# Q, K, V and output projections as column tiles beside PV, in a one-core transformer block (adaLN, sliding-window attention, gMLP)

## The chip, the cores and the metric

The kernel runs on one core of a Trainium2 chip. The metric is the time of one execution in microseconds (us); three runs of the kernel before took 271.88, 272.19 and 272.67 us, median 272.19.

A core has five engines that work side by side and wait for each other by semaphores: PE multiplies matrices (and loads their stationary operand, shown as PEld), ACT evaluates functions and copies, DVE and POOL work elementwise, SP issues most of the DMA transfers. A matmul streams the columns of a moving operand past a stationary one and writes sums into one of eight banks of an accumulator, `ps`; ACT and DVE copy results out. The 128 x 128 array can also be used in parts: row tiles (here four of 32 rows, of which 28 are used) or column tiles (four of 32 columns), each with its own stationary operand.

## The reference

The input x has 2048 rows of 448. With six vectors made from the condition c:

```
mod = silu(c) @ w_mod                      # sa, ca, ga, sb, cb, gb
h = layernorm(x) * (1 + ca) + sa
q, k, v = split(h @ wqkv)                  # 16 heads of 28
p = softmax(q @ k.T / sqrt(28), over the last 256 keys up to the row itself)
x = x + ga * ((p @ v) @ wo)
h = layernorm(x) * (1 + cb) + sb
z1, z2 = halves of gelu(h @ w_in)          # 896 + 896
g = w_sp @ layernorm(z2) + b_sp            # 2048 x 2048 over the rows
out = x + gb * ((z1 * g) @ w_out)
```

Inputs and output are bfloat16, sums are float32.

## The kernel before, in words

**Tiling.** The rows are cut into 16 tiles of 128. Attention goes tile by tile: tile j needs the keys of tiles j-2, j-1 and j. For each pair (tile, key tile) there are 16 score matmuls (one per head; four heads at a time as row tiles, `s_mm`, L806), two exponentials of 128 x 1024 on ACT (L841, one for half of the heads each), a mask on POOL for the first and last key tile (L847), and 16 PV matmuls as column tiles (`pv_fn`, L852, 128 rows x 32 columns, a column of ones in `Vaug` gives the softmax's sum). Then DVE transposes and normalises (L873 to L882), and `wo` multiplies (L889, result added to x at L892).

**Before attention.** The rows are normalised (L557 to L579), transposed to `hT` (blocks 0 to 2, that is tiles 0 to 3, by PE with an evacuation that applies the modulation, L629 to L648; the others by DMA, L663) and modulated. `project` (L719) computes Q and K transposed, eight groups of four heads per block, with `WQK` as the stationary operand and `hT` as the moving one, and V with `hT` as the stationary one, in chains of four steps over 448 = 4 overlapping chunks of 128 (rows that stand twice are zero in one of the chunks, L506 and L507). `WQK` has 32 columns for every head of 28, so that each head's Q and K land at a multiple of 32 partitions; eight copies (L679 on DVE, L680 on ACT) make it out of the loaded `wqk_raw`.

**After it.** LN and modulation again (`h2`), z1 and z2 by `w_in` with gelu (`Pair`, L684; rests of 64 rows as two row tiles at L711), the large product G (L1027, 448 matmuls of 512 columns), the elementwise product (L1037, L1039), `w_out` and the sum `fin` (L1059), one store per tile (L1061). The `w_in` products fill PE during attention where its order has room, and the rest of them follows. `w_sp` comes transposed by DMA (L1008); its second half overwrites `Vaug` and `PT` and waits for the last PV.

**Start.** The loads of c, x, w_mod, wqkv stand at L472 to L493; PE runs 30 matmuls on zeros (`warm`, L1068) so that it is busy before there is data. `mod_cols` (L526) makes sa and ca as 8 columns with four steps each, for which both halves of `w_mod` (L476) have to be there.

**Order.** No engine reorders its work: the program lists every operation, and `ORDER` (L164) gives the one order in which all are emitted, with a bank or buffer after "/" and the engine after "." where there is a choice. Each engine executes its own operations in that order, and `emit` (L102) puts in the waits. All matmuls but one kind go through `mm` (L438), so the profile shows nearly all of PE's work under L439.

Of the kernel before, what the change touches and what calls it, by code (L numbers as in the profile page):

```python
# [5 lines left out]
BF16 = mybir.dt.bfloat16  # L6
# [5 lines left out]
SWITCH = 95  # L12
# [43 lines left out]
class Planner:  # L56


    def __init__(self):
        self.ops = []  # L60
        self.last = {}
        self.order = []

# [15 lines left out]
    def schedule(self):  # L79
# [20 lines left out]
        assert len(self.order) == len(set(o.seq for o in self.order)) == len(self.ops)  # L100

    def emit(self, sems, dma_sems):  # L102
# [17 lines left out]
        for o in self.order:  # L120
# [18 lines left out]
            if o.dma is not None:  # L139
                dcount[name] = dcount.get(name, 0) + 16  # L140
                tok = ("dma:" + name, dcount[name])
                prog[eng].append(("op", o.fn, tok[0], 16))
                dlast[name] = tok
            else:
                cnt[eng] += 1
                tok = (eng, cnt[eng])
                prog[eng].append(("op", o.fn, eng, 1))
# [6 lines left out]
    def run(self, eng, e):  # L154
        for item in self.prog[eng]:
            if item[0] == "wait":
                e.wait_ge(self.sems[item[1]], item[2])
            else:
                _, fn, key, inc = item
                fn(e).then_inc(self.sems[key], inc)  # L160
# [4 lines left out]
0 32 14 24 29 20 1693/0 22 1694 21 34 33 35/1 1695 1696 1 2 55 4 113 114 1697 25 23 56 57 1698 1699 1700 1701 1702 1703 3 1704 26 31 36 38/0 37 1705  # L165
1706 1707 115 30 116 117 58 59/1 39 40 41 42 8 170 43 44 45 46 10 64/4 9 168 169 118.2/4 65 1708 119/1 1709 1710 62/1 1711 1712 11 63 121/0 122 171
120.1 60/4 61.1 1713 1714 1715 1716 16 50 1717 48.1 1718 1719 1720 66/2 13 1721 1722 67 49 47 78/3 128/3 79 73/4 74 54 75 76 53 83/6 84 172 80 51 52.1
5 173 85 86 12 81 77 68/1 87 82 129 69 70 71 72 143/2 144 239 240 174 175/2 237 145 7 130 146 147 131 132 153/0 154 484/0,0 133/1 134 135 136 137.1
148/2 149 155 156 150 151 177/3 176.1/3 178 157.1 486/1 233 98/7 28 99 100 152 101 487 179 123/0 124 125 126 127.1 234 93/1 94 95 96 102.1 97.1 27
103/2 6 104 105 106 107.1 235 238 236 241 18 322 88/0 89 90 91 92 242 243 244/4 138/0 19 139 140 141 245.1/1 142 485/0,0 320 399 108/2 109 110 111  # L170
489/2 158/1 159 160 112 181/3 161 162 180 182 482/2 15 501/1,0 505/4 401 246.1/3 402 198/1 17 199 163/0 164 200 201 165 247.1/2 166 403 202.1 203/3
204 205 206 193/1 194 195 196 502/7 508/1,0 207 218/3 219 167 483 220 188/0 221 248 222.1 189 190 191 192.1 249 197 183/1 184 185 186 213/2 214 187.1
215 216 217.1 509/3 208/3 209 506 511/8 318 210 488/0 323 503 490 491 492/0 493 494.1/1 522/0,1 523/9 211 212.1 526/1 251 228/1 319 223/2 224 225 229
250 230 231 232 316 317 226 227 252 507/0 253 254 321 324 512 510 504 255 529/1,0 530/3 276/3 405 513/0 266/1 267 268 261/2 262 325 326 327/2 331
330.1/3 269 533/10 527 270 277 329/0 263 264 524 536/1,0 539/5 537/0 334 278 279 280.1 271/0 272 311/1 265.1 273 312 514 313 314 274 275.1 550/1,0
296/3 328.1/1 315 297 298 299 300.1 515.1/0 404 406 256/1 257 291/0 258 259 400 407 551/4 552 557/1,2 292 293 294 554/6 260.1 286/1 287 288 289 561/8
564/2,0 516/2 295.1 538/0 558/2 534 540 535 525 528 495/1 408 409 531 532 555 562 332 559 290.1 281/1 282 567/7 578/0,1 283 284 541/0 517/0 518 542
543.1/0 565/3 285.1 579/1 519 520 585/0,2 333 335.1 336.1 544/0 496/1 497 498 499 582/0 917 521 560/0 563 566 568 553 556 337 500 589/10 586/5 569/0
570 592/2,1 593/3 914 545/1 546 547 548 916 412.1/3 369/0 370 371 338.1 583 947 349/3 350 945 549 372 373.1 595/8 606/0,1 607/6 351 610/9 352 364/1
587 365 366 367 353.1 946 613/0,2 915 588/0 614/7 571.1/0 572/1 590 591 596 580 581 584 368.1 594 354/1 355 356 620/0,1 597/0 573/0 574 575 410.1/1  # L180
416 948 949 615 576 617/4 344/2 931/3 577 345 346 347 621/1 623/10 608 357 611 358 413.1/0 960 348.1 962 932 598 950 933 920 634/1,0 934 935 936 414
937 938 618 635/0 306/1 307 411/2 308 309 939 641/1,2 599.1/0 301/0 302 1426 303 304 417 310.1 384/1 638/8 385 386 387 961 600/0 922 645/5 648/0,2 963
964 965 305.1 616/0 619 609 388.1 612 646 622 624 339/1 340 642/3 651/2 662/1,2 639 341 342 636 625/0 637/0 652 649/6 650 643 644 647 640 626 627.1/1
415 418.1 420.1 663/1 669/0,1 343.1 359/1 360 361 362 653/0 374/0 375 376 377 666/7 667 664 673/5 676/1,2 654 670/9 671 679/4 363.1 601/1 602 603
628/2 378.1 629/0 677/3 630 631 951 952.1/1 923 632 633 690/2,0 691/0 421.1 966 604 694/2 605 389/0 390 391 392 697/1,2 394/1 395 396 419.1 967/0
698/10 393.1 442/0 397 919 701/8 398.1 674 443 444 445 704/1,0 655.1/0 379/1 380 446.1 672/0 675 702 975 1428 381 382 953 954/1 955 656/0 383.1 707/6
718/2,0 705/5 665 722/1 699 723 680 678 719/4 668 681/0 657/1 658 682 683.1/0 720 659 660 661 990 991 725/1,0 726/3 727 729/7 730 437/0 438 439 440
452/1 441.1 959.1 976 453 454 455 732/1,2 724/0 721 456.1 728 432/1 433 434 435 977 978 436.1 735/9 746/0,2 684/0 918 969/1 731 733/1 968 695 692 736
734 979 422/1 423 424 425 737/0 738 739.1/1 750/3 753/1,2 685/0 686 687 688 426.1 747/1 447/1 958.1 957.1 754/9 755 757/4 970 740/2 760/0,1 763/7 751
448 689 992 449 450 451.1 693/0 708 761/6 696 927 700 703 706 709/0 774/1,2 778/10 972 427/1 428 429 430 467/0 468 710 469 470 775/2 781/2,0 785/5  # L190
431.1 472/1 473 471.1 711.1/0 762/0 782/6 758 759 752 756 993 764 748 749 994 788/1,0 791/7 971 1430 789/1 474 475 1425 765/0 457/0 924 458 459 776
460 802/0,2 476.1 741/1 742 743 744 980 461.1 462/0 463 464 465 766 973.1 803/4 809/0,1 995 996 712/2 745 713/1 783 714 806/3 715 716 466.1 786 787/0
792 767.1/0 810/0 816/0,2 779 768/1 981 982.1/1 984/2 790 784 813/9 814 928 717 929 1432 777 921 819/5 780 793/0 956.1 794 769/1 770 771 772 773
830/2,1 817/1 926 940/0 831/6 834/8 925 1065/1 1067 1066 1071/3 1068 1069 1070 1073.1 1005 930 941 837/1,0 1081/2 942 1084/3 983 999/0 1000 795.1/0
838/10 841/2 1082 1085 1086 1083 807 1087 1089.1 835 804 944 943 818/0 796/0 1072 815 997/1 844/0,1 847/9 808 811 812 805 820 1088 832 797/1 798 799
800 858/1,2 821/0 477/0 822 478 801 845/7 1429 479 859/0 839 480 1022 481.1 842 974.1 1097/1 1098 1099 1007 1008 823.1/1 985 988.1 865/0,1 843/0 986.1
1006 1009 998 1003.1 1002 1001.1 840 862/4 833 846 1101/2 866/3 867 1010 836 848 849/0 850 869/7 1113/3 824/0 851/1 870 863 1100 1102 1103 1105.1
872/0,1 873/10 1114 875/5 1115 1117/0 1020 1021 1104.1 825/2 826 827 1116 1119 1118 1011 1121 1014/1 886/1,0 887/8 828 1317/3 1319 876/0 868 874 852/2
1120 853/3 854 855 829 1322/0 1023 1012/0 1013 890/6 893/1,0 897/1 856 857 1024 1318 871 860 864 861 1323 1320 1308/1 1310 1004 894/3 900/0,1 1025
877/0 1026 1029.1/2 1321 1309 989 987 1344/2 1345 1346 901/10 1173/0 1178 903/9 1175 1027.1/0 878 879/1 1035 1036 1015 1016.1 1174 1037 1176 1145/1  # L200
1146 1150 1017.1 888 891 1148 1177 1149 1019 1147 1151 1179 1324 1314/3 1313 1311 1038 1325 1347/0 1348 1180/0 1152/2 1312 1316 1326/5 1315 1181 1349
1335/4 1338/6 1339 1337 1182 898 1331/7 1350 1351 1332 1341 1330 1328 1352 1039 1183 1184 880/0 1040 1433 1129/1 1154 1018.1 899/0 1153 902 1030 892
904 895 896 889 1028 1031 1033 1034 1032 1427 881/2 1451 1131 882 1041 1042/1 1329 905/0 1044/2 1122/1 1123 1106/3 1132/3 1185 1124 1327 906 907.1/1
1371/2 1373 1336 1107 1334 883 1333 884 885 1108 1340 1186 1343 1155 1156 1372 1133 1342 1130 1125 1126 1043 1157 1376/5 1375 1201/1 1202 1374 1045
# [55 lines left out]
def mm_ns(n):  # L260
    return n / 2.4 + 3.0


def act_ns(n):
    return 52 + 0.8333 * n
# [18 lines left out]
def bass_adaLN_cond__sliding_block__mixer_gmlp__prompt_kernel(  # L284
# [153 lines left out]
    def mm(e, out_, lhsT, rhs, st, sp, **kw):  # L438
        return e.matmul(out_, lhsT=lhsT, rhs=rhs, start=st, stop=sp, **kw)  # L439
# [688 lines left out]
```

## Time and profile before

| | |
|---|---|
| median of three runs | 272.19 us |
| profiled execution | 271.65 us |
| its span on the core | 269.9 us |
| PE, DVE, ACT, POOL busy | 260.3, 171.8, 132.0, 101.2 us |
| 90 exponentials (L841) | mean 1034 ns |
| 720 score and 720 PV matmuls of 128 columns | mean 217 and 222 ns |
| matmuls of 512 columns, `ps<-hT,WQK` | mean 380 ns |
| granted PE clock over the span | 1.00 |

The span runs from the first to the last instruction of the kernel's own program. A matmul's row in the profile lasts until its result is out, and the next one starts long before that; so the sum of the rows says little, and the distance between starts says what a matmul takes of PE. The stretches and timelines of the profile give starts; the rows of single forms give means.

### The profile page before, as it was taken

Reading aid. Unit: us, or ns where it says so; the run is one execution under the profiler, and the core shown is the slowest. Engines: PE = TensorE matmul, PEld = TensorE weight load, DVE = VectorE, ACT = ScalarE, POOL = GpSimd, SP = SyncE. Lnnn points to the kernel's source line nnn. Section 1 sums busy time; section 2 is a strip of 40 time slices with the busy share of each in tenths; the row PEclk is TensorE's granted clock in tenths of the full one; section 3 lists DMA queues with packets and bytes.
Section 4 is the critical chain, followed back from the end, with each engine's and each line's share of the span. In section 5 each row is a group of like instructions: output and inputs, shape, how many; then the busy total and the mean of one; then the engine's idle time right before and its main releaser. Section 6 shows DMA issues by size and latency. Waiting matters only on the chain.

```text
span 269.9 us, 6339 instructions
## 1 busy us (share of the span) xinstructions
PE 260.3 (96%) x2660; PEld 126.4 (47%) x2689; DVE 171.8 (64%) x413; ACT 132.0 (49%) x177; POOL 101.2 (37%) x160
## 2 busy tenths in 40 slices
PE   7989999999999999999999999999999999999995
PEld 2756445554544454344444444444444444444553
DVE  5789989778889998798986723115242132265444
ACT  5688999999999998986675300000000001000000
POOL 3174789798879996575322300000000000000000
PEclk9999999999999999999999999999999999999999
DMA  7955163691679421637599991000000000000214
GB/s 222 343 188 72 22 163 89 82 163 22 75 122 305 74 52 26 111 73 123 116 220 181 184 192 31 2 0 0 0 2 0 0 0 2 17 0 0 69 53 137
DMA packets 60811, 23.85 MB, mean 88 GB/s; under 512 B 49839, under 2 KB 60654, under 8 KB 60782
## 3 DMA queue, kind: packets, MB, share of 16 engines
q1 hardware_dynamic: 60507, 22.98, 40.9%
q10 hardware_dynamic: 274, 0.46, 0.6%
q8 instruction: 21, 0.34, 0.5%
q14 instruction: 9, 0.07, 0.1%
HBM read 9.53 MB, written 1.84 MB: 42 GB/s over the span
## 4 chain that ended last, share of the span: by engine, by line
PE 79%; DVE 9%; ACT 5%; POOL 3%; issue 2%; DVEq 0%; POOLq 0%
PE ps L439 79%; ACT PT L841 5%; DVE w_out_sb L897 1%; DVE QKT L743 1%; POOL PT L847 1%; POOL hT L655 1%; DVE hT L655 1%; DVE st_all L557 1%; DVE wo_sb L788 1%; DVE oq L873 1%; POOL xn L578 1%; DVE WQK L679 1%; DVE ve_all L564 1%; DVE xn L578 0%; DVE Vaug L754 0%
## 5 line engine op out<-in xcount | busy, mean ns | idle before, releaser
L841 ACT ACTIVATE PT<-ps 128x1024 bf16<-128x1024 f32 x90 | 84.9, 1034 | 3.9 <-PE ps L439 3.5
L1037 DVE TENSOR_TENSOR tmpg<-ps,bsp_bc 128x512 bf16<-128x512 f32 x28 | 18.8, 687 | 58.8 <-PE ps L439 58.6
L968 ACT ACTIVATE z1T<-ps 128x512 bf16<-128x512 f32 x28 | 15.4, 600 | 79.6 <-PE ps L439 79.6
L439 PE MATMUL ps<-QKT,z 128*128 128x512 bf16 x223 | 51.2, 379 | 0.1
L847 POOL TENSOR_SCALAR_AFFINE_SELECT PT<-PT 128x512 f32<-128x512 f32 x60 | 37.5, 647 | 4.0 <-ACT PT L841 3.9
L565 POOL TENSOR_TENSOR rs_all<-ve_all,neghalf 128x1 f32<-128x1 f32 (+2 forms) x30 | 19.9, 666 | 39.1 <-DVE ve_all L564 39.0
L439 PEld LDWEIGHTS ps<-QKT,z 128*128 128x128 bf16 x224 | 21.8, 98 | 26.4 <-ACT z1T L968 0.3
L439 PE MATMUL ps<-hT,WQK 128*128 128x512 bf16 (+2 forms) x179 | 30.9, 304 | 3.0 <-issue 0.8
L439 PE MATMUL ps<-w_in_sb,hT 128*128 128x448 bf16 (+1 forms) x128 | 29.2, 354 | 0.1
L439 PE MATMUL ps<-hT,w_in_sb 128*128 128x512 bf16 (+1 forms) x105 | 27.1, 380 | 0.4 <-DVE hT L655 0.2
L439 PE MATMUL ps<-w_spD,z 128*128 128x512 bf16 x110 | 26.4, 379 | 0.2
L439 PE MATMUL ps<-w_spC,z 128*128 128x512 bf16 x106 | 25.8, 379 | 0.3
L439 PE MATMUL ps<-w_out_sb,z1T 128*128 128x448 bf16 (+2 forms) x119 | 21.5, 342 | 0.0
L557 DVE BATCH_NORM_STATS2 st_all<-z2raw 128x6 f32<-128x448 bf16 x32 | 18.8, 610 | 3.7 <-ACT z2raw L949 2.3
L439 PEld LDWEIGHTS ps<-hT,WQK 128*128 128x128 bf16 x192 | 14.4, 97 | 13.1 <-DVE QKT L743 1.2
L557 DVE BATCH_NORM_STATS2 st_all<-x_sb 128x6 f32<-128x448 bf16 x32 | 19.4, 614 | 1.5 <-DMA x_sb<-in_A_x_dram 1.4
L743 DVE CAST QKT<-ps 128x512 bf16<-128x512 f32 (+2 forms) x34 | 18.5, 558 | 2.6 <-PE ps L439 2.5
L439 PE MATMUL ps<-QKT 28*128 28x128 bf16 x720 | 18.3, 217 | 0.8 <-ACT QKT L740 0.5
L1059 DVE TENSOR_TENSOR fin<-ps,x_sb 128x448 bf16<-128x448 f32 (+2 forms) x17 | 9.8, 595 | 13.6 <-PE ps L439 10.5
L439 PEld LDWEIGHTS ps<-QKT 28*128 28x128 bf16 x720 | 10.4, 92 | 15.3 <-ACT PT L841 10.3
L439 PEld LDWEIGHTS ps<-w_in_sb,hT 128*128 128x128 bf16 (+1 forms) x128 | 10.2, 96 | 15.5 <-issue 5.9
L439 PEld LDWEIGHTS ps<-w_spC,z 128*128 128x128 bf16 x112 | 11.0, 98 | 13.2
(75 smaller groups left out, 304.5 us busy)
## 6 DMA issues: line engine op xcount, KB each, us to landing
wmod_sb<-in_w_mod_dram SPq DMA_DIRECT2D x8, 224.0 KB, 4.6
w_in_sb<-in_B_w_in_dram SPq DMA_DIRECT2D x8, 224.0 KB, 3.2
out_dram<-fin SPq DMA_DIRECT2D x16, 112.0 KB, 1.8
x_sb<-in_A_x_dram SPq DMA_DIRECT2D x3, 448.0 KB, 7.6
wqk_raw<-in_A_wqkv_dram SPq DMA_DIRECT2D x2, 452.0 KB, 6.0
bsp_bc<-in_B_b_sp_dram SPq DMA_DIRECT2D x1, 512.0 KB, 4.2
wmod_sb<-in_w_mod_dram ACTq DMA_DIRECT2D x1, 448.0 KB, 4.1
wmod_sb<-in_w_mod_dram SPq DMA_DIRECT2D x1, 448.0 KB, 4.9
```

Of the source, the lines that this page charges most:

```text
L439: return e.matmul(out_, lhsT=lhsT, rhs=rhs, start=st, stop=sp, **kw)
L557: st = [dve("%sst%d" % (name, i), prio, dve_ns(D), lambda e, i=i, s_=s_: e.bn_stats(st_all[:, slot, t, i, :], s_()), deps, tens) for i, s_ ...
L564: v = dve(name + "ve", prio, 75, lambda e: e.tensor_scalar(ve_all[:, slot, t0:t1], mv_all[:, slot, t0:t1, 1], EPS, None, ALU.add), deps)
L565: r = pool(name + "rs", prio, 420 + 148 * n, lambda e: e.tensor_tensor(rs_all[:, slot, t0:t1], ve_all[:, slot, t0:t1], neghalf[:, t0:t1], ...
L578: return e.tensor_scalar(dst, src, rs_all[:, slot, t:t + 1], nm_all[:, slot, t:t + 1], ALU.mult, ALU.add)
L655: return e.tensor_scalar(hT[:, c_, cols], hT[:, c_, cols], modT[:, base_col + 4 + c_:base_col + 5 + c_], modT[:, base_col + c_:base_col + ...
L743: return e.tensor_copy(QKT[:, g, cols], ps[:, ten.slot, 0:w])
L841: e_op = P.op("E%d_%d" % (j, ui), pr, [("act", 925, lambda e, e_in=e_in, e_out=e_out: e.activation(e_out(), e_in(), ACT.Exp, scale=SCALE)) ...
L847: ready = pool("M%d_%d" % (j, ui), pr - 50, pool_ns(512), lambda e, pt=pt, pat=pat, cm=cm, cmp=cmp: e.affine_select(out=pt32(pt.slot), in_ ...
L968: g = P.op("z1g%d_%d" % (tb, ft), pr - 19, [("act", act_ns(512), lambda e: e.activation(z1T[:, ft, tb * 512:(tb + 1) * 512], ps[:, ten.slo ...
L1037: a = dve("ga%d_%d" % (tb, ft), pr, dve_ns(512), lambda e, tb=tb, ten=ten, tg=tg: e.tensor_tensor(tmpg[:, tg.slot, :], ps[:, ten.slot, :], ...
L1059: fs.append(dve("fin%s%d" % (nm, t), pr, dve_ns(c1 - c0), lambda e, t=t, ten=ten, ft_=ft_, c0=c0, c1=c1: e.tensor_tensor(fin[:, ft_.slot, ...
```

## The change

Five things change together.

- Q and K: `WQK` and its eight copies go. `mm_heads` takes the 28 columns of each head (and the 4 next to them) straight out of `wqk_raw` as the stationary operand of a column tile, so a step of 128 columns becomes four matmuls of 32 columns, each with the whole moving operand. The chain runs over chunks 2, 3, 0, 1 and waits for each half of the load by itself.
- Other matmuls near PV: `column_tiles` looks along PE's order. Where a run of plain matmuls, PV and QK is not broken by scores, 64-row rests, modulation or warming, and holds at least one PV or QK, every plain matmul in it is emitted as four column tiles, too. By the program's order there are 2016 column tiles (720 of them PV) instead of 720, and 854 whole matmuls instead of 1185; row tiles stay as they are.
- The first modulation is summed in two passes, first the second half of `w_mod` for all 8 columns, then the first half.
- Loads: the second half of wqk comes right behind w_mod's, then x tile 1, x tiles 2 and 3, wqk's first half, x tiles 4 to 11, then wv (two loads instead of three, zero rows cleared by POOL after the load).
- `ORDER` is new as a whole: which engine evacuates what, which bank is used, and where every operation stands. 23 warming matmuls instead of 30.

```diff
+FREE, COLS, WHOLE = 128, 33, 129
+    def column_tiles(self):
+        seg = []
+        for o in [o for o in self.order if o.eng == "pe"] + [None]:
+            if o is not None and o.mode in (FREE, COLS):
+                seg.append(o)
+                continue
+            if any(x.mode == COLS for x in seg):
+                self.cols.update(x.seq for x in seg)
+            seg = []
...
     def mm(e, out_, lhsT, rhs, st, sp, **kw):
+        if P.col and "tile_position" not in kw:
+            for j in range(4):
+                last = e.matmul(out_[32 * j:32 * j + 32], lhsT=lhsT[:, 32 * j:32 * j + 32], rhs=rhs, start=st, stop=sp,
+                                tile_position=(0, 32 * j), **kw)
+            return last
         return e.matmul(out_, lhsT=lhsT, rhs=rhs, start=st, stop=sp, **kw)
...
+    t_wmA[0].order = [x0]
+    t_wmA[1].order = [t_c]
+    t_wqk = load_dup("wqk", -97, wqk_raw, A_wqkv, 0, 904, order=t_wmA)
+    t_wqk[0].order = [t_wqk[1]]
+    x0b = load_x("x0b", -96, 1, 1, [t_wqk[1]])
+    t_wv = load_dup("wv", -95, wv_sb, A_wqkv, 2 * D, 3 * D, o=2 * D, order=[x0b])
+    x1 = load_x("x1", -96, 2, 2, [x0b])
...
-    z_qk = dve("zqk", -67, 480, lambda e: e.memset(WQK[0:64, 2, :, :], 0.0))
+    z_qk = P.op("zqk", -67, [("dve", 480, lambda e: e.memset(wqk_raw[0:64, 2, :], 0.0)), ("pool", 600, lambda e: e.memset(wqk_raw[0:64, 2, :], 0.0))], [t_wqk[1]])
...
-    t_modA, m1 = mod_cols("modA", -50, (0, 1), 0, t_wmA, CH, 128)
+    for h in (1, 0):
+        for col in range(8):
+            def fn(e, h=h, i=col // 4, mc=col % 4, col=col):
+                last = None
+                for kc in (2 * h, 2 * h + 1):
+                    last = mm(e, ps[:, mA_ten.slot, col:col + 1], wmod_sb[:, kc, i * D + CH[mc]:i * D + CH[mc] + 128], sc_sb[:, kc:kc + 1],
+                              h == 1 and col == 0 and kc == 2, h == 0 and kc == 1, skip_group_check=True)
+                return last
...
-            t_wqkp[gp].append(P.op("wqkf%d_%d" % (gp, c_), -45 + gp * 10, [
-                ("dve", 205, lambda e, d=dst, s_=src: e.tensor_copy(d, s_)),
-                ("act", act_ns(512), lambda e, d=dst, s_=src: e.activation(d, s_, ACT.Copy)),
-                ("pool", 620, lambda e, d=dst, s_=src: e.tensor_copy(d, s_))][0:2 if r0 else 3], t_wqk, port=True))
...
+    def mm_heads(e, out_, lhsT, rhs, st, sp):
+        for j in range(4):
+            last = e.matmul(out_[32 * j:32 * j + 32], lhsT=lhsT[:, DH * j:DH * j + 32], rhs=rhs, start=st, stop=sp,
+                            tile_position=(0, 32 * j))
+        return last
...
-            for k in range(4):
+            for k in (2, 3, 0, 1):
...
-    for i in range(30):
-        n_ = 512 if i < 12 else 256
+    for i in range(23):
+        n_ = 512 if i < 9 else 256
```

## The prediction

> **What bounds the kernel now.** I read the page's busy times first, then the busy time by stretches of 10 us, then PE's timeline in a stretch where the three kinds of matmul meet, and last ACT's timeline at the end of attention.
>
> ```profile
> PE 260.3 (96%) x2660; PEld 126.4 (47%) x2689; DVE 171.8 (64%) x413; ACT 132.0 (49%) x177; POOL 101.2 (37%) x160
> ```
> ```profile
> 20.00:30.00 10.00, 9.68 (x150) 5.85 (x153) 9.86 (x26) 9.05 (x14) 4.51 (x6) 1.00 0.36 54
> ...
> 70.00:80.00 10.00, 9.44 (x201) 4.83 (x204) 8.93 (x21) 10.00 (x12) 8.51 (x14) 1.00 0.84 115
> 80.00:90.00 10.00, 9.60 (x216) 4.88 (x219) 8.83 (x20) 9.98 (x12) 9.26 (x14) 1.00 0.87 224
> ...
> 100.00:110.00 10.00, 9.65 (x159) 4.22 (x162) 8.64 (x24) 8.79 (x11) 6.99 (x11) 1.00 0.19 40
> ```
>
> The columns are PE, PEld, DVE, ACT, POOL. PE looks full everywhere, but a matmul row lasts until its data is out, so I price PE by the distance from one start to the next: 216 ns for 512 columns, 189 for 448, 109 for 256, 56 for 128. From 120 us on these distances fill the time: PE alone bounds that part. From 50 to 90 us ACT is idle 0.1 us in 40: there the exponentials (one per 0.912 us) set the pace, and PE has holes that its long rows cover.
>
> ```profile
> 65.72 0.38 PE L439 MATMUL ps<-hT,WQK 128*128 128x512 bf16 x1
> 66.03 0.40 PE L439 MATMUL ps<-QKT 28*128 28x128 bf16 x16
> 66.37 0.55 PE L439 MATMUL ps<-wv_sb,hT 128*128 128x448 bf16 x2
> 66.89 0.41 PE L439 MATMUL ps<-PT,Vaug 128*32 128x128 bf16 x16
> 67.23 0.55 PE L439 MATMUL ps<-wv_sb,hT 128*128 128x448 bf16 x2
> 67.72 0.40 PE L439 MATMUL ps<-QKT 28*128 28x128 bf16 x16
> 68.05 0.65 PE L439 MATMUL ps<-PT,Vaug 128*32 128x128 bf16 x32
> ```
>
> "128*32" is a column tile: all 128 rows, 32 columns; "28*128" is a row tile (scores); "128*128" the whole array. 65.72 to 66.03 is 0.31 us for one matmul of 512 columns, 0.095 more than 0.216. Every change between the three kinds costs this: the median from start to start is 311 ns (512 columns, then scores), 309 (512, then PV), 146 (scores, then whole), 150 (PV, then whole). The order of the program has 146 such changes, 13.9 us in all.
>
> ```profile
> 104.24 1.94 ACT L841 ACTIVATE PT<-ps 128x1024 bf16<-128x1024 f32 x2
> 106.69 1.94 ACT L841 ACTIVATE PT<-ps 128x1024 bf16<-128x1024 f32 x2 [0.51 <-PE ps L439]
> 109.13 1.94 ACT L841 ACTIVATE PT<-ps 128x1024 bf16<-128x1024 f32 x2 [0.51 <-PE ps L439]
> ```
>
> At the end of attention it is the other way round: ACT waits for PE, 0.51 us per pair.
>
> I therefore split the span at PE's scores. Scores of tile 1 start at 19.0 us, the last scores at 108.7, the last matmul ends at 266.8, and fin and store take 3.1 more: 269.9. By the prices above, PE's work between the two is 73.0 us of matmuls and 118 changes (11.2), 84.2 in 89.7; behind the last scores it is 157.4 in 158.1. ACT from tile 1's first exponential (19.4) to the 89th (109.1): 86 x 0.912 + 6.5 of evacuations (L740 2 x 0.405 and 2 x 0.628, L751 4 x 0.553, L942 4 x 0.554) = 84.9 of 89.7; by the stretches 3.8 us are idle, 2.2 between 20 and 50 us, 1.5 after 90.
>
> **The change, part by part.**
>
> *Column tiles.* In the new order 324 whole matmuls of QK, V, wo, transposes, gate and w_in become 1296 column tiles, four to one. Does a group of four keep the pace of the one? PV is the row that shows it: 32 of them take 0.65 us including a tail of 0.22, 14 ns each, 56 per four, which is the whole array's 56 ns at 128 columns; their 32-column weight loads lie under that. So I add 0 per group. The bounds: a gain has no ground, since the same columns stream; the loss is at most 0.164 us, if each group of 512 ran out (its row is 0.380) before the next began. Changes fall from 146 to 121: 25 x 0.095 = 2.4 us of PE; scores still need two changes each.
>
> The Trainium skill, page "TensorE: Matmul & The Clock Gate", section "Measured speedup vs the span model", speaks against this: it gives three column tiles 2.38 times one, not 3. By that a group of 512 would take an estimated 216 x 3 / 2.38 = 272 ns, 56 more, and the 240 groups of 256 to 512 columns up to 13 us more instead of 0; PV's 56 ns per four does not bear it out, though at 128 columns only.
>
> *Weights as loaded.* Gone: six copies on DVE (6 x 0.29), two on ACT (2 x 0.64) and a DVE memset of 0.49. PE waited for these copies: the first QK starts at 11.40, behind a 0.67 us gap that a copy ended. What is late next: hT of tile 0 (before until 10.4 on ACT) and the second half of wqk. Landings before: x0 2.85, wmod 5.41 and 6.59, wqk 8.37 and 9.58, x2 11.08, that is 0.46 MB per 1.2 us. At that pace, in the new order (x0, wmod, wqk half, x0b, x1, wqk half, x2): 7.5, 7.8, 8.4, 9.6, 11.1. The first four chains end near 10.3. The zero rows are now a POOL memset behind the wqk landing: 904 elements against `warm`'s 512 in 0.52 give 0.93 us, done at 8.5, hidden by hT; if that half came last, +0.6. wv's zeros (0.46) stand behind the first mask on POOL; wv lands near 13 behind x3, the first V is near 16; uncovered, up to +1 for the POOL work behind it.
>
> ACT then does three evacuations, two hT (0.4 each) and the first exponential at about 11.9 instead of 13.3. But before the second one stand xn (0.81) and ten evacuations (0.223 apart): 11.9 + 0.92 + 0.81 + 2.3 = 16.0, and scores behind them 0.3: 16.3 against 16.6. So of 1.4 us only about 0.3 is left, and at tile 1 I take 0.4; bounds -1.0 and +1.0 (x0b lands 3.9 us later than before, and stats, POOL's rs and hT of tile 1 hang on it).
>
> *Modulation in two passes, fewer warm matmuls.* 3 x 0.427 of 512-column warming go, but six of 256 (0.213 from start to start there, 0.109 only from 8.5 us on) now stand ahead of the first pass: it begins at 6.9 as before, and the second ends near 8.55, as before. 0; the wait for the second wmod half (6.59) is hidden behind the first pass, and costs what that half is late.
>
> *New order.* PE between tile 1's scores and the last: 71.1 + 94 x 0.095 = 80.0 (4.2 less: 2.3 of changes, 1.9 of work). Behind the last: 159.1, which is 1.65 more. ACT in its stretch: 3 x 0.405 + 0.553 + 5 x 0.628 + 2 x 0.554 = 6.0, 0.5 less. Two z1T (0.6) and two more table loads (1.28) now stand before the last exponential, 3.8 us: its PV comes about 113, but PE has 11.2 us of work after the last scores before it asks for that: hidden by 4. POOL gets 3.6 us more (hT +4.1 -2.3, xn +3.2, o_sb -2.8, memsets +1.4) and DVE 3.1 less; POOL has 16 us free between 20 and 110, so 0, at worst +1 through masks. On SP, the transposes of w_sp that need all PV move behind other ones: some 22 after the last hT transpose (130.5 before) at 1.31 us end near 160; PE asks for the first w_spD near 162 and w_spC near 169: 0, at worst +2.
>
> **The sum.** End = last scores + 159.1 + 0.7 + 3.1. ACT sets the last scores over most of the way, so they move by 0.4 (start) + 0.5 (less ACT work) + the part of ACT's 3.8 us idle that goes. After 90 us PE needs 14.9 us for the last eight scores instead of 17.5, so the 1.5 idle there goes; of the 2.2 early I take 0.6. 3.0 in all: 105.7 + 162.9 = 268.6, that is -1.3 on 269.9. The profiled execution took 271.65 with what lies around the span, so 270.3; the median of the runs is 0.54 above it: **270.8**.
>
> **Rivals.**
> - *PE bounds all of attention.* Then the whole 4.2 counts: last scores -4.6, end -2.95: 269.2. For it: PE looks 96% busy, and ACT waits for it at the end. Against: ACT's 0.1 us idle from 50 to 90.
> - *The work moved behind the last scores comes out at the end (slower).* If ACT keeps its 3.8 us idle and the start gives nothing, the last scores move by 0.5 only, and 1.65 us more work follows: +1.15, 273.3. It decides whenever the last scores come less than 1.65 us earlier. For it: ACT already has no slack for 40 us, DVE 9.86 of 10 from 20 to 30, and in the early part ACT's own work grows (up to the 72nd exponential 4.9 against 4.3). Against: the 0.51 us waits are PE's.
> - *Groups of four do not keep pace.* If the next group's four loads did not fit under the current group, each group would cost a PV group more, 56 ns. 207 of them lie between tile 1's scores and the last: 80.0 + 11.6 + 1.5 idle = 93.1 instead of 89.7, less 0.4 for the start; 33 behind: 1.85. 3.0 + 1.65 + 1.85 = +6.5: 278.7. It decides once a group costs about 29 ns more (240 groups x 29 ns = the 7 us that PE has over). The Trainium skill's rule above is this case. Against: PV's 14 ns. The program then does not do what it says.
>
> **How the numbers follow.** Forecast 0.48, PE bound 0.17, slower by moved work 0.25, slow groups 0.07, nothing moves 0.03. About 0.3% (0.8 us) is what a measurement of this kernel can tell from no change. The forecast's own spread of 1 us gives 0.40 faster and 0.08 same; with PE bound 0.17, a fifth of the slower case as same, and the rest: faster 0.57, same 0.14, slower 0.29. The range runs from 268.8 (PE bound, with the start's better bound in part) to 273.4 (moved work); outside lie the slow groups and the tails.
>
> **What would show it.** Column rows of 512: start of x28 to the next row near 28 x 54 ns right, over 60 wrong. First exponential near 11.9, the one before tile 1's near 16.3. ACT idle from 90 to 110 under 0.6 us. Last scores at 105.7; at 107 or later the slower case holds, at 104.1 the PE case. A gap on PE behind w_spD or w_spC would make the end wrong.

## The result, and the profile after

The changed kernel took 279.01 us (median of four runs, 278.38 to 279.33) where the kernel before took 272.04 beside it: a ratio of 1.0249, 95% interval 1.0224 to 1.0274. It is slower by 7.0 us; the forecast was 270.8, and the range (268.8 to 273.4) does not hold it. The profiled execution took 278.96 us, its span 276.9.

Cut where the prediction cut the span, at PE's scores:

| profiled execution | before | after | forecast | measured |
|---|---|---|---|---|
| first exponential starts | 13.31 | 11.74 | 11.9 | 11.7 |
| exponential ahead of tile 1's | 16.60 | 20.93 | 16.3 | 20.9 |
| scores of tile 1 | 18.99 | 23.61 | -0.4 | +4.6 |
| from there to the last scores | 89.69 | 89.44 | -2.6 | -0.25 |
| behind the last scores, to the end of the span | 161.25 | 163.86 | +1.65 | +2.6 |

Two thirds of the loss are there by 23.6 us, ahead of the whole stretch that the prediction spent most of its words on. The page of the kernel after, its busy times, its granted clock and its queue of instruction transfers:

```profile
PE 261.2 (94%) x3639; PEld 130.4 (47%) x3654; DVE 171.5 (62%) x399; ACT 133.2 (48%) x178; POOL 105.1 (38%) x167
...
PEclk9968999999999999999999999999999999999999
...
q8 instruction: 28, 0.46, 0.7%
```

The same line in the kernel before:

```profile
q8 instruction: 21, 0.34, 0.5%
```

PE has 979 more matmuls on record and is busy 0.9 us longer only, so the column tiles do not look dear here. What is new is a dip in the clock (third and fourth digit, 13.8 to 27.7 us) and, on a line that I had not read, 28 packets of instructions of 16 KB (0.46 MB in all) where the kernel before has 21. Late packets of the kernel before start at 173.02, 200.50, 228.31 and 255.25 us, and between them lie 255, 257 and 267 matmuls and weight loads of PE, so one packet holds some 256 instructions.

PE's timeline of the start (start, length, line, shapes, count, and idle time before the row with what ended it):

```profile
11.90 1.26 PE L739 MATMUL ps<-hT,wqk_raw 128*32 128x128 bf16 x70 [0.36 <-ACT hT L670]
16.46 1.89 PE L739 MATMUL ps<-hT,wqk_raw 128*32 128x128 bf16 x62 [3.30 <-issue]
...
18.47 1.48 PE L739 MATMUL ps<-hT,wqk_raw 128*32 128x128 bf16 x44
```

and two rows of the same work in the kernel before, as whole matmuls:

```profile
11.40 1.63 PE L439 MATMUL ps<-hT,WQK 128*128 128x128 bf16 x26 [0.67 <-DVE WQK L679]
...
14.29 1.51 PE L439 MATMUL ps<-hT,WQK 128*128 128x128 bf16 x24
```

After the change PE stops for 3.30 us in the middle of one run of the same matmuls, and "issue" says that it waited for no semaphore. Behind the stop everything takes twice as long: 44 tiles in 1.48 us where 70 had taken 1.26. The stretches show why (columns as in the prediction, the granted clock behind POOL):

```profile
12.00:14.00 2.00, 1.16 (x70) 0.92 (x69) 2.00 (x7) 1.63 (x3) 1.42 (x3) 1.00 1.14 316
14.00:15.50 1.50, 0.00 (x0) 0.00 (x0) 0.72 (x5) 0.00 (x0) 1.02 (x2) 0.99 1.06 284
15.50:22.30 6.80, 5.38 (x150) 4.07 (x153) 3.45 (x9) 3.11 (x10) 1.25 (x2) 0.50 0.23 78
22.30:24.00 1.70, 1.70 (x68) 0.99 (x60) 1.12 (x4) 1.47 (x4) 1.29 (x2) 1.00 0.79 69
```

The clock is halved 2.3 us after PE ran dry (its last row ends at 13.16) and comes back 5.8 us after it goes on. During the stop, up to 15.5 us, the DMA engines are full (a share above 1); while the clock is halved they are not (0.23).

Now the stretches that answer to those shown of before, and the timeline where the kinds meet:

```profile
80.00:90.00 10.00, 9.42 (x277) 4.69 (x266) 9.01 (x21) 9.85 (x12) 7.21 (x11) 1.00 0.02 7
...
100.00:110.00 10.00, 8.49 (x205) 4.44 (x202) 8.58 (x19) 9.27 (x12) 6.68 (x10) 1.00 0.19 40
```
```profile
62.92 1.05 PE L739 MATMUL ps<-hT,wqk_raw 128*32 128x512 bf16 x16
63.80 0.40 PE L454 MATMUL ps<-PT,Vaug 128*32 128x128 bf16 x16
...
65.39 1.05 PE L739 MATMUL ps<-hT,wqk_raw 128*32 128x512 bf16 x16 [0.51 <-DVE QKT L766]
66.26 0.93 PE L451 MATMUL ps<-wo_sb,oT 128*32 128x448 bf16 x16
```

From 50 to 90 us ACT is nearly as full as before (0.95 us idle in these 40 instead of 0.1). And the column tiles keep pace: 65.39 to 66.26 is 0.87 us for 16 of them, four groups of 512 columns at 0.217 us each, which is the whole matmul's 0.216; and 62.92 to 63.80 is 0.88 for four groups with PV right behind them, so that change costs no 95 ns. Over the whole trace, the median from the start of the last group of 512 columns of Q and K to the PV matmul behind it is 216 ns, where the whole matmul took 309. Last, ACT at the end of attention:

```profile
100.91 7.49 ACT L865 ACTIVATE PT<-ps 128x1024 bf16<-128x1024 f32 x8
109.01 3.77 ACT L865 ACTIVATE PT<-ps 128x1024 bf16<-128x1024 f32 x4 [0.61 <-PE ps L454]
113.50 1.02 ACT L865 ACTIVATE PT<-ps 128x1024 bf16<-128x1024 f32 x1 [0.72 <-PE ps L454]
```

The waits of 0.51 us per pair are gone, two others have come. PE's own waits there are for DVE's evacuations of z (L963, 1.1 us).

**The theories.** A: PE's instructions come in pieces of 256 over the same DMA engines as the loads. A group of four column tiles takes eight instructions (four loads of weights, four matmuls) where a whole matmul takes two, and at 128 columns a group lasts 56 ns: PE uses up what it has before the next piece is there. B: it is the new order or the new loads that stop PE. C: column tiles of 128 columns are slow in themselves.

### The profile page after: what moved, and what is told of

It is laid out like the page before. It is cut to its first block, busy times and chain, and to the rows that moved or that the text cites. A ratio compares the mean times of both kernels' runs of the same rounds, so it can differ in the third digit from the quotient of the medians.

```text
span 276.9 us, 8285 instructions
## 1 busy us (share of the span) xinstructions
PE 261.2 (94%) x3639; PEld 130.4 (47%) x3654; DVE 171.5 (62%) x399; ACT 133.2 (48%) x178; POOL 105.1 (38%) x167
## 4 chain that ended last, share of the span: by engine, by line
PE 66%; DVE 12%; SPq 11%; ACT 3%; DMA 3%; issue 3%; POOL 1%; DVEq 0%
PE ps L454 50%; SPq L1032 10%; PE ps L451 8%; PE ps L739 8%; DVE st_all L586 3%; ACT PT L865 2%; DMA x_sb<-in_A_x_dram 2%; DVE oq L897 1%; DMA w_spD<-in_B_w_sp_dram 1%; DVE QKT L766 1%; DVE x_sb L916 1%; DVE hT L684 1%; POOL xn L607 1%; DVE Vaug L778 1%; DVE o_sb L902 1%
## 5 line engine op out<-in xcount | busy, mean ns | idle before, releaser
L454 PE MATMUL ps<-QKT,z 128*128 128x512 bf16 x219 | 49.6, 379 | 0.3
L739 PE MATMUL ps<-hT,wqk_raw 128*32 128x512 bf16 (+2 forms) x768 | 35.9, 322 | 4.7 <-issue 3.3
L454 PE MATMUL ps<-w_spC,z 128*128 128x512 bf16 x109 | 24.7, 379 | 0.2
L454 PE MATMUL ps<-hT,w_in_sb 128*128 128x512 bf16 (+1 forms) x90 | 23.0, 380 | 0.5 <-issue 0.3
L739 PEld LDWEIGHTS ps<-hT,wqk_raw 128*32 128x32 bf16 x768 | 17.0, 103 | 13.7 <-issue 3.5
L454 PE MATMUL ps<-w_in_sb,hT 128*128 128x448 bf16 (+1 forms) x104 | 22.7, 353 | 0.2 <-issue 0.2
L607 POOL TENSOR_SCALAR xn<-x_sb,rs_all,nm_all 128x512 bf16<-128x512 bf16 x23 | 18.4, 808 | 8.9 <-DVE nm_all L624 5.5
L586 DVE BATCH_NORM_STATS2 st_all<-z2raw 128x6 f32<-128x448 bf16 x32 | 18.7, 612 | 2.5 <-ACT z2raw L973 2.4
L766 DVE CAST QKT<-ps 128x512 bf16<-128x512 f32 (+2 forms) x27 | 15.6, 580 | 4.7 <-PE ps L739 4.6
L454 PEld LDWEIGHTS ps<-w_spD,z 128*128 128x128 bf16 x112 | 10.9, 98 | 14.1 <-DMA w_spD<-in_B_w_sp_dram 1.1
L684 POOL TENSOR_SCALAR hT<-hT,modT 128x256 bf16<-128x256 bf16 (+1 forms) x28 | 17.0, 614 | 0.9 <-DMA hT<-xn 0.9
```

The lines of the kernel that those rows point to most:

```text
L586: st = [dve("%sst%d" % (name, i), prio, dve_ns(D), lambda e, i=i, s_=s_: e.bn_stats(st_all[:, slot, t, i, :], s_()), deps, tens) for i, s_ ...
L607: return e.tensor_scalar(dst, src, rs_all[:, slot, t:t + 1], nm_all[:, slot, t:t + 1], ALU.mult, ALU.add)
L684: return e.tensor_scalar(hT[:, c_, cols], hT[:, c_, cols], modT[:, base_col + 4 + c_:base_col + 5 + c_], modT[:, base_col + c_:base_col + ...
L739: last = e.matmul(out_[32 * j:32 * j + 32], lhsT=lhsT[:, DH * j:DH * j + 32], rhs=rhs, start=st, stop=sp, tile_position=(0, 32 * j))
L766: return e.tensor_copy(QKT[:, g, cols], ps[:, ten.slot, 0:w])
```

## The experiments

All ratios are to the kernel before, run on the same chip. Line numbers of an experiment's own kernel differ a little from those of before and after.

**1. start_whole: the kernel after, with Q and K of tiles 0 and 1, and the plain matmuls between them, as whole matmuls.** A whole matmul takes 128 neighbouring columns as stationary operand, so three of four heads of these two tiles get shifted columns; the columns streamed, the loads and the order stay.

```diff
-lambda k, g=g: wqk_raw[:, k, 112 * g:112 * g + 116], lambda k: hT[:, k, cols], w, COLS, mm_heads)
+(lambda k, g=g: wqk_raw[:, k, min(112 * g, 776):min(112 * g, 776) + 128]) if b < 2 else (lambda k, g=g: wqk_raw[:, k, 112 * g:112 * g + 116]),
+lambda k: hT[:, k, cols], w, WHOLE if b < 2 else COLS, mm_near if b < 2 else mm_heads)
```

(`mm_near` emits one whole matmul.)

> The kernel after, but Q and K of the first two tiles (steps of 128 columns) are whole matmuls again: one instruction pair instead of four, with 128 neighbouring columns of the loaded weights as stationary operand, and the plain matmuls between them are whole again too. Three of four heads of these two tiles so get Q and K from shifted columns; the number of columns streamed, all loads and the order are those of after. Theory A (supply of instructions): column tiles of 128 columns take eight instructions per 56 ns instead of two, PE uses up what has been fetched (it stopped after some 463 instructions at 13.2 us) while the next 16 KB piece waits behind the loads. Then the 3.30 us idle put down to 'issue' is gone (under 0.3), the granted clock stays 1.0 from 15 to 22 us, the second exponential starts near 16.5 instead of 20.93, tile 1's scores near 19 instead of 23.61, and the time falls by 4.0 to 4.8 us: 274.2 to 275.0. Rival B (the new loads and order cost the start): the idle stays, in whatever form, and the time stays within 1 us of 279. Rival C (PE simply takes longer for 128-column tiles, no gap): the time falls by 1 to 2 us only.

Measured: 273.44 us (nine runs), 1.0074 (1.0051 to 1.0098); against the 1.0249 of the kernel after that is 4.8 us less. PE's timeline where the kernel after stops:

```profile
12.21 2.09 PE L744 MATMUL ps<-hT,wqk_raw 128*128 128x128 bf16 x33 [0.34 <-ACT hT L670]
...
14.40 0.78 PE L744 MATMUL ps<-hT,wqk_raw 128*128 128x128 bf16 x11
16.02 0.29 PE L454 MATMUL ps<-QKT 28*128 28x128 bf16 x8 [0.84 <-DVE hT L675]
```

132 tiles have become 33 matmuls and run without a stop, the clock is 1.00 throughout, the second exponential starts at 16.36 and tile 1's scores at 19.43. Loads and order are those of the kernel after, so B falls for the 4.8 us. Of the 2.0 us that are left over the kernel before, tile 1's scores account for 0.44.

**2. before_cols_start: the kernel before, with nothing but tiles 0 and 1 as column tiles.**

```diff
-ops, ten = chain("qk%d_%d" % (b, g), ..., lambda k: hT[:, k, cols], w)
+ops, ten = chain("qk%d_%d" % (b, g), ..., lambda k: hT[:, k, cols], w, mm4 if b < 2 else mm)
```

(`mm4` emits the four column tiles of one step.)

> The kernel before, with one part of the change: Q and K of the first two tiles as four column tiles per step out of the padded copy; loads, order, modulation and all else as before. Theory A: 60 steps of 128 columns before 18 us now take eight instructions instead of two, 360 more; PE runs out of instructions between 13 and 16 us, an idle put down to 'issue' of 1.5 to 3.5 us appears, the clock is halved behind it, and the time rises by 2.5 to 5 us: 274.7 to 277. Rival B (new loads and order): no such idle, time within 0.5 us of 272.0. Rival C (column tiles only slower by themselves): +0.5 to +1.5 without a gap.

Measured: 277.68 us, 1.0219 (1.0187 to 1.0251): 5.9 us more, and so more than the 2.5 to 5 us expected.

```profile
12.85 0.68 PE L721 MATMUL ps<-hT,WQK 128*32 128x128 bf16 x35
17.88 0.37 PE L721 MATMUL ps<-hT,WQK 128*32 128x128 bf16 x5 [4.34 <-issue]
```

This one edit makes the stop in the old order and with the old loads, and a longer one than expected (4.34 us; 1.5 to 3.5). It also shows that it is a matter of a count. Matmuls and weight loads done up to the stop, in this kernel, in the kernel after, and in late_loads (below), each from the span's start to a time within the stop:

```profile
0.00:15.00 15.00, 11.37 (x221) 6.79 (x222) 10.61 (x37) 9.17 (x20) 5.03 (x18) 1.00 0.91 288
```
```profile
0.00:14.00 14.00, 9.89 (x221) 5.79 (x222) 8.27 (x30) 7.53 (x16) 5.94 (x20) 1.00 0.90 298
```
```profile
0.00:13.50 13.50, 10.30 (x221) 6.07 (x222) 8.18 (x30) 7.53 (x16) 5.73 (x19) 1.00 0.71 240
```

Three kernels with different matmuls, and at different times PE stops after the same 221 matmuls and 222 loads: 443 instructions on record, at most some 463 with the waits that the program's order puts between them. It would be two pieces of 256 if what the engine runs ahead of the kernel's first instruction takes some 50 more; the trace doesn't show that part, so the two pieces are an inference.

**3. late_loads: the kernel after, with the loads behind wv held back.**

```diff
+for o in P.ops:
+    if o.name == "wmodG1":
+        o.deps.append(next(q for q in P.ops if q.name == "qke1_6"))
```

(In `ORDER`, the loads of w_mod's gate columns, x tiles 8 to 15 and wo stand behind that evacuation, the statistics of these tiles later.)

> The kernel after, with the loads that stand behind wv (gate columns of w_mod, x tiles 8 to 15, wo; 1.8 MB) held back until an evacuation of tile 1's Q and K (about 15 us) is done, and the statistics of x tiles 8 to 15 a little later on DVE; nothing else. Theory A1 (the fetch waits behind loads): the first instruction packet of PE starts near 12 instead of 13.69 us, the idle put down to 'issue' falls from 3.30 to under 1.5 us, the half clock goes or shrinks, and the time falls by 2 to 5 us (274 to 277), less what the held loads cost later. Theory A2 (the fetch is late by itself, loads do not matter): idle of 3.0 to 3.3 us stays and the time is 278.5 to 280. Rival B (order) also expects 279 or more.

Measured: 281.62 us, 1.0372 (1.0336 to 1.0407). The time is a miss, by 5 us and more. At the start it went as A1 has it: the first packet of PE's instructions starts at 11.33 us instead of 13.69, and

```profile
11.62 1.26 PE L741 MATMUL ps<-hT,wqk_raw 128*32 128x128 bf16 x70 [0.36 <-ACT hT L672]
13.84 1.07 PE L741 MATMUL ps<-hT,wqk_raw 128*32 128x128 bf16 x62 [0.96 <-issue]
...
17.54 0.23 PE L456 MATMUL ps<-QKT 28*128 28x128 bf16 x2 [0.92 <-issue]
```

0.96 us at the same place instead of 3.30, no halved clock there, tile 1's scores at 20.21, 3.4 us earlier than after. But the held loads took all of it back and more: DVE stands 4.1 us for wo,

```profile
DVE wo_sb L814 <- DMA wo_sb<-in_A_wo_dram: 4.1, 1, 4.1
```

PE stops behind it for 3.1 us, and the clock is halved from about 27 to 37 us in the profiled execution; the stretch from tile 1's scores to the last takes 97.4 us instead of 89.4. So the loads make the stop longer, and they are not all of it: with the first packet 2.4 us earlier, 0.96 and 0.92 us of idle stay.

**4. late_run_128 and late_run_256: the price of a piece by itself.** In the kernel before, 36 matmuls of G near 200 us become column tiles of 128 or 256 columns; no load runs there, and PE alone sets the time.

```diff
+    def mm4(e, out_, lhsT, rhs, st, sp):
+        for c in range(0, 512, 128):
+            for j in range(4):
+                last = e.matmul(out_[32 * j:32 * j + 32, c:c + 128], lhsT=lhsT[:, 32 * j:32 * j + 32], rhs=rhs[:, c:c + 128], ...)
+        return last
...
-                        last = mm(e, ps[:, ten.slot, :], ...)
+                        put = mm4 if (tb, ft, qd) in RUN else mm
+                        last = put(e, ps[:, ten.slot, :], ...)
```

> The kernel before, with one stretch of 36 matmuls of 512 columns in the large product G (L1027, near 200 us, where PE alone sets the time and no load runs) written as column tiles of 128 columns: 16 column tiles for one matmul, 576 of them, 1152 instructions in 7.8 us, the same columns and sums. Theory A with numbers from the traces (a piece is 256 instructions; PE asks for the next one when it has used one up; packet 1.0 to 1.2 us, and 1.5 us more until PE went on): at full pace 256 such instructions last 1.73 us, a piece takes 2.5 us or a little more, so PE stops for 0.8 to 1 us at each of four or five pieces, rows of 'issue' idle without any load in the way, and the time rises by 3.0 to 4.5 us. Rival A3 (only the loads make the piece late): no idle, time within 0.5 us of before. Rival C (a column tile of 128 columns is slow in itself): a rise without gaps.

> The same 36 matmuls as column tiles of 256 columns: 288 tiles, 576 instructions, 256 of them in 3.47 us. Theory A: a piece (2.5 to 2.7 us) is there before it is needed; no 'issue' idle over 0.2 us, time within 0.4 us of before (two changes of kind, 0.2). A supply that is limited by the number of instructions only from 512 columns down, or a dearer group of four (56 ns each, 72 groups: +4 us), would show as a rise of 1 us or more.

Measured: 279.43 us, 1.0284 (1.0255 to 1.0313), and 272.04 us, 1.0012 (1.0001 to 1.0022). PE's timelines, first with 128 columns:

```profile
199.66 2.30 PE L724 MATMUL ps<-QKT,z 128*32 128x128 bf16 x150
203.43 1.97 PE L724 MATMUL ps<-QKT,z 128*32 128x128 bf16 x128 [1.46 <-issue]
206.88 1.97 PE L724 MATMUL ps<-QKT,z 128*32 128x128 bf16 x128 [1.48 <-issue]
210.88 1.97 PE L724 MATMUL ps<-QKT,z 128*32 128x128 bf16 x128 [2.03 <-issue]
214.61 0.79 PE L724 MATMUL ps<-QKT,z 128*32 128x128 bf16 x42 [1.76 <-issue]
```

then with 256:

```profile
199.88 8.04 PE L724 MATMUL ps<-QKT,z 128*32 128x256 bf16 x288
```

All that the DMA engines moved in the first of the two kernels from 198 to 217 us:

```profile
DMA packets 5, 0.08 MB, mean 4 GB/s; under 512 B 0, under 2 KB 0, under 8 KB 0
...
q8 instruction: 5, 0.08, 1.8%
```

The first timeline is theory A drawn out: between two stops lie exactly 128 tiles, 256 instructions, one piece. They are done in 1.73 us (128 tiles, 32 groups at 54 ns; the row's 1.97 has the last one's way out in it), and the next piece is there 3.45, 4.00 and 3.73 us after the one before it. The four stops make 7.7 us from end to start of the work, and the kernel is 7.7 us slower (0.0284 x 271.6). A3 and C fall: no load is near, and 54 ns per group is full pace. My number for a piece, 2.5 us, was too small, so the expected 3.0 to 4.5 us was, too: the trace's records show 1.05 us from the first use of a piece (203.43) to the start of the next packet (204.48), 1.0 for the packet, and 1.4 until PE goes on (205.47 to 206.88). With 256 columns a piece lasts 3.47 us, about as long as the next one takes: no stop in this stretch of little more than two pieces, and 0.3 us more for two changes of kind and little else.

**5. What the later column tiles bring: before_cols_late and all_whole.** before_cols_late is the kernel before with the pass of the change (`column_tiles`) from tile 2 on, Q and K of tiles 0 and 1 whole; all_whole is the kernel after without that pass and without `mm_heads`.

```diff
+                for o in ops:
+                    o.mode = 129 if b < 2 else 33
...
+    P.column_tiles()
```
```diff
-lambda k, g=g: wqk_raw[:, k, 112 * g:112 * g + 116], lambda k: hT[:, k, cols], w, COLS, mm_heads)
+lambda k, g=g: wqk_raw[:, k, min(112 * g, 776):min(112 * g, 776) + 128], lambda k: hT[:, k, cols], w, WHOLE, mm_near)
...
-    P.column_tiles()
```

> The kernel before, with the other part of the column tiles: Q and K from tile 2 on (256 and 512 columns) and the plain matmuls near PV and near these as four column tiles each; Q and K of tiles 0 and 1 whole; order, loads, weight copies as before. My prediction's step: a group of four costs as much as one matmul and each change of kind that goes saves 95 ns of PE. If ACT alone sets the pace of attention, 0 to -0.3 us; if PE's saved changes count behind 90 us only, about -1 (271.0); if PE bounds all of attention, about -2.5 (269.5). Slow groups (my rival, 56 ns per group): +4 or more. Theory A adds: no 'issue' idle over 0.3 us, since the pieces are used up more slowly (256 columns and more per group) and the loads are over.

> The kernel after with no column tiles at all but PV: Q and K of every tile whole (128 neighbouring columns as stationary operand, so three of four heads get shifted columns) and all other matmuls whole; loads and order as after. Beside start_whole (column tiles from tile 2 on, 1.0074 of before) it shows what these bring: by the program's order 25 and more changes of kind of 95 ns come back. If ACT sets attention's pace: 0 to +1 us on start_whole (1.007 to 1.011 of before). If PE bounds it: +2.4 us or more (1.016). If column tiles were slow in themselves: below start_whole.

Measured: 272.27 us, 1.0024 (1.0005 to 1.0043), and 275.29 us, 1.0132 (1.0111 to 1.0153). In the old order the column tiles save 22 of 146 changes of kind and bring nothing: the time is 0.65 us longer, where the smallest of the expected effects was a gain of 0 to 0.3. The stretch of attention takes 90.4 us there instead of 89.7, with the same 86.4 us of ACT's work; tile 1's scores start 0.7 us earlier in that execution (18.28) and the last ones at the same 108.7. What holds them there I did not settle. In the new order they save 40 changes (160 to 120, 3.8 us of PE), and all_whole is 1.6 us slower than start_whole, between the two expected branches; its stretch of attention is 1.9 us longer. So the changes of kind that went were worth some 40% of their price in the new order and nothing in the old one. That PE is late in the one and ACT sets the pace in the other would explain it, but no run here separates this from other differences of the two orders.

Taken one after the other, the parts of the change are (in us, ratio times 272): new order and loads, with all matmuls whole, +3.6; column tiles from tile 2 on, -1.6; column tiles in tiles 0 and 1, +4.8. Their sum is the measured +6.8 by construction, since each is the difference to the one ahead of it in this row; put on the old order, they cost +0.65 and +5.9. Of the +3.6, 2.65 us lie behind the last scores (163.90 instead of 161.25).

**6. wsp_order: the end.** In the kernel after, two transposes of w_spC move behind the last five of w_spD in `ORDER`:

```diff
-... 1446 ... 1441 ... 1449 ... 1453 ... 1452 ... 1454 ... 1450 1661/7 ...
+... 1449 ... 1453 ... 1452 ... 1454 ... 1450 1441 1446 1661/7 ...
```

> The kernel after with two of SP's 32 transposes of w_sp (of w_spC) moved behind the last five of w_spD, which so start 2.6 us earlier; nothing else. If the queue of SP holds the end (PE stands 0.65 us for w_spD at 171.5 us), the wait goes and the span behind the last scores falls from 163.86 to 163.0 to 163.3. If not, it stays at 163.8 to 163.9 and another wait takes its place.

Measured, in one run: 278.85 us, and behind the last scores 163.02 us instead of 163.86. PE's timeline after, then in this kernel:

```profile
169.85 1.03 PE L454 MATMUL ps<-w_spD,z 128*128 128x512 bf16 x4
171.52 2.76 PE L454 MATMUL ps<-w_spD,z 128*128 128x512 bf16 x12 [0.65 <-DMA w_spD<-in_B_w_sp_dram]
```
```profile
170.57 3.62 PE L456 MATMUL ps<-w_spD,z 128*128 128x512 bf16 x16
```

The wait is gone and no other has come. late_loads, with the transposes where the kernel after has them, also takes 163.02 us behind its last scores and has no wait for w_spD: its attention took 8 us longer, so the queue had the time. Both fit a queue of SP that is late. The whole time hides this, since this run's start happened to be later (tile 1's scores at 24.64); the stretch is what can be read.

**7. repaired: the kernel after with both cures.** The edits of 3 and 6, with wo ahead of x tiles 12 to 15 this time and the statistics near their old place.

> The kernel after, complete, with what the runs so far point to, and column tiles everywhere as in after: the gate columns of w_mod, x tiles 8 to 15 and wo held back until tile 1's Q and K are evacuated, but wo ahead of x tiles 12 to 15 this time and the statistics of x near their old place (in late_loads DVE stood 4.1 us for wo); and the two transposes of w_sp moved as in wsp_order. Theory A: a piece of 256 instructions is used up in 1.8 us by column tiles of 128 columns and takes 3.5 to 4 us without loads, so some 'issue' idle stays (0.9 to 2 us in all, as in late_loads), tile 1's scores start near 20.2 instead of 23.61, the clock is not halved; the end gains 0.8 more: 274.0 to 276.0, still over the kernel before. If it is 278 or more, the held loads cost elsewhere what they give at the start. If it is under 273, the supply of instructions was all that was wrong with this start.

Measured: 278.11 us, 1.0237 (1.0186 to 1.0288); the profiled execution took 277.76. Tile 1's scores start at 20.12 and the end takes 163.03, both as expected, and the clock is 1.00. But the time misses the expected 274.0 to 276.0: the stretch of attention takes 92.6 us, 3.1 more than after: in the first 10 us behind tile 1's scores ACT is busy 7.33 us (9.47 after), and PE waits 1.5 us for DVE's product with wo. It is the expected branch "278 or more": held loads cost elsewhere what they give at the start. None of the kernels with the new order beats the kernel before; start_whole, 2.0 us over it and with shifted columns for most heads of two tiles, came nearest.

## Why the prediction was wrong, point by point

**The step that failed** is the one on the start: "So of 1.4 us only about 0.3 is left, and at tile 1 I take 0.4; bounds -1.0 and +1.0". It priced the column tiles of 128 columns by their columns alone, with "I add 0 per group" taken over from PV, and never asked what 1296 matmuls and as many weight loads in place of 324 each take of PE's supply of instructions. In attention PV comes in bursts of 8 to 32 tiles (16 to 64 instructions), so its 14 ns each could not show it; Q and K of tiles 0 and 1 are 256 tiles, up to 132 in a row. PE ran out of instructions and stopped for 3.30 us at 13.2, and the halved clock followed; the step cost 4.8 us (after against start_whole). Without it the step holds: in start_whole the second exponential starts at 16.36 (forecast 16.3) and tile 1's scores 0.44 us later than before, within the bounds.

- *Groups of four keep pace*: right at the pace (0.217 us per 512, 54 ns per 128 within a piece); at 128 columns only as long as the instructions last. The rival of slow groups named the measured total within 0.3 us, for a reason that didn't occur; the estimate of 272 ns per group by the Trainium skill, page "TensorE: Matmul & The Clock Gate", section "Measured speedup vs the span model", is not borne out: that section is on the span of one pack, and a stream of packs kept the pace here.
- *The supply of instructions* is no term of the prediction. The Trainium skill, page "Runtime: NRT & Kernel Launch", section "Instruction fetch mechanics", says that instructions come through a FIFO that is refilled in blocks of 256, and calls the cost of crossing a block mostly hidden. The blocks agree with late_run_128's rows of 128 tiles; hidden they are only while a block lasts longer than the 3.45 to 4.0 us that the next one takes. The same section gives TensorE room for 2048 instructions and also speaks of two blocks only; PE runs dry after 443 to 463 instructions in these traces, which fits the two blocks better.
- *Weights as loaded, first exponential*: right, 11.74 for 11.9. Modulation and warming: no loss shows in start_whole.
- *Attention, -2.6*: a size that was off, by 2.35. ACT's work fell by 0.37 us (0.5 forecast), but its idle time did not go: 3.4 us of 89.7 before, 3.5 of 89.4 after. (The prediction's prices leave 4.8 us idle before, its stretches 3.8; the busy time between the two scores, 86.3 us, leaves 3.4.) In the last part (94.4 to 113.05) ACT is idle 1.24 us; PE, which I had freed there, now waits for DVE's z. In "after 90 us PE needs 14.9 us for the last eight scores instead of 17.5, so the 1.5 idle there goes" the first half is borne out in kind (PE is busy 16.5 us of the last 18.65, before 18.4 of 18.7) and the conclusion is not: it looked at PE's work alone and for no wait of PE.
- *Behind the last scores, +1.65*: measured +2.6. 0.8 us of it is the wait for w_spD that I set at 0 with a worst case of 2; without it, in wsp_order, the end is 1.77 us longer than before, close to the 1.65 forecast for the work. The 22 transposes behind the last one of hT were counted right, but they took 34.8 us (137.36 to 172.15) instead of 28.8, some 1.58 us each and not 1.31, and they began 6.9 us later than in the kernel before (the last scores come 4.4 us later).
- *The sum*: 5.0 + 2.35 + 0.95 = 8.3 us between forecast and result on the span, -1.3 and +7.0.
- *The rival of moved work* had the right mechanism for the rest: with the start's 4.8 us taken out, the kernel is 2.0 us slower (start_whole), where that rival said 1.15: the last scores come 0.24 us earlier than before, and 2.4 us more follow them.

## What to carry to other kernels

Count instructions as well as columns: a form that computes the same with four times as many instructions also uses up its supply four times as fast, and what can be sustained here is 256 instructions per 3.5 to 4 us, a group of four column tiles (eight instructions) per 108 to 125 ns, less while loads fill the DMA engines. An idle "issue" in the middle of a run of equal matmuls is the sign, and the profile's line of instruction packets is the place to look, before the change as well as after it. And where an engine is freed, look for what it waits for next before you give its time to the path.

## What the runs showed of the hardware

- PE fetches its instructions in packets of 16 KB over the DMA engines that carry the loads. In the kernel after, the first packet started at 13.69 us, 3.0 us after PE's 256th matmul or load on record (10.70), and took 1.25 us; with the loads held (late_loads) it started at 11.33, 0.9 us after the 256th.
- Stops of 1.5 to 2.0 us, four in 15 us, did not touch the granted clock (1.00 in late_run_128). Those of 3.1 (late_loads), 3.3 (after) and 4.3 us (before_cols_start) halved it, in the kernel after from 15.5 to 22.3 us, and from 2.3 us after PE ran dry. The halvings on record last 6.83 or 10.24 us, two or three times 3.41; in the 3.41 us ahead of one, PE was idle for 1.9 us in late_loads (24.74 to 26.65), 2.3 in the kernel after and all 3.4 in before_cols_start, so a stretch that was idle in part was enough. The Trainium skill, page "TensorE: Matmul & The Clock Gate", section "What's actually happening", puts the limit at one idle window of about 3.4 us; these traces show the halving with less idle time than that.
- A column tile of a neighbouring shape costs no change of kind: in the kernel after, the median from the start of a group to the start of what follows is 216 ns from Q and K (512 columns) to PV or to V, and 189 ns from V (448 columns) to PV and from wo to Q and K, the same as within a run of one shape.
